# A PSUM bank for each copy of the first x tile, the activation table load behind w1's issues, the last w1 gradient in halves, and a new set of planner constants

## The chip, the cores and the metric

The kernel runs on one core of one Trainium2 chip. The time is the device time of one execution in microseconds (us). The engines are TensorE (PE, with its weight loads PEld), VectorE (DVE), ScalarE (ACT), GpSimd (POOL) and SyncE (SP, which here only issues DMAs).

## The reference

The kernel computes the output and all gradients of a small speech network: two strided convolutions, each followed by GELU, and a joint of the frames with eight label states.

```python
B, T, D, K, U = 2, 16000, 256, 3, 8          # all inputs bf16
# forward
h = gelu(conv(x, w1))[:, ::2]                # kernel width 3
f = gelu(conv(h, w2))[:, ::2]                # [2, 4000, 256]
fe = f @ w_f;  ge = g @ w_g
j = tanh(fe[:, :, None] + ge[:, None])       # [2, 4000, 8, 256]
out = j @ w_o                                # [2, 4000, 8, 256]
# backward, from grad_out of the shape of out
return out, grad_x, grad_w1, grad_w2, grad_g, grad_w_f, grad_w_g, grad_w_o
```

## The kernel before

**Tiling.** The 8000 output frames of both batches are cut into chunks: the first has 256 frames, fifteen have 512 (of these, one holds the border of the two batches), the last has 64. One chunk runs through three stages. `stage_a` loads x transposed into `XC` (by a DMA transpose; for the first chunk rows are loaded and TensorE transposes them, in `rows_xc`), makes both convolutions with GELU and its derivative (`conv_gelu`: g_sq, g_s, G1o, G1e, G2), and fe. `stage_j` handles the eight label states in four pairs (`pair(up)`): JT is tanh(fe+ge), `OUT` is JT times w_o, `GOT` is grad_out transposed by DMA, NGZ/ZS/NGP collect the gradient through tanh, `JR` is JT with frames on partitions, and `gwo` sums w_o's gradient into the bank `GWO`. For the first two chunks JR comes from TensorE transposes of JT (L688), later from a DVE add and an ACT tanh (L694, L699). `stage_de` goes back through both convolutions: GN, GH, their DMA transposes GNR and GHR, the weight gradients (`wgrad`, accumulated in ACC1, ACC2 and ACCF) and the gradient of x (`GX`).

**The order of the work** is made at build time by a planner, `Flow`. Each step is an `op` with an engine (or a choice of two, mostly ACT or DVE), a modelled cost, the tiles that it reads and writes, and a due time (`at`, or `F.now`). Times of `at` are in frames: a chunk of 512 frames is 512 long, `dt` is the chunk's length, `q` a quarter of it, one pair's time. `Flow.issue` runs a model of the engines: of the steps whose inputs are done and whose buffer is free it takes the one that can start first, and among those that can start at the same time the one due first. The result is a fixed list of instructions for each engine. On the chip an engine runs its list in order and waits where an input is missing. SP's list is chosen in the same model, with one DMA ring: `TURN` holds the pause between kinds of transfers (T transpose, L load, S store), `BACKLOG` how far SP may run ahead.

**PSUM.** Seven banks are handed out as class `ps` in any order; the eighth is GWO. An ACT and a DVE instruction that read the same bank run one after the other on the chip; the model before does not know that.

**Start.** L1174 zeroes a tile, 20 matmuls on it (`warm_up`) run while the first x travels. ACT issues the loads of w1 (three), w_f, w_g and w_o, and then loads its function table with a small GELU (L1175). In `rows_xc` the halves of x come one after the other: eight TensorE transposes (L388) into one bank, two copies of that bank into XC (L324 on ACT, L329 on DVE), and filler matmuls (`unread`, FILL of them) behind each half's transposes.

**End.** `last_w1(i)` makes the gradients of w1's three taps for the last two chunks at once. Its result, 256 x 256, fills one bank, a DVE instruction adds ACC1 to it (L901, `acc_add` with `final`), and a store of 128 KB follows. The last chunk's four GX copies (L326, L331) and two stores are due around it (`late`).

Of the kernel before, what the change touches and what calls it, by code (L numbers as in the profile page):

```python
# [20 lines left out]
class Buf:  # L21


    def __init__(self, cls, shape, dtype, name):
        self.cls, self.shape, self.dtype, self.name = cls, shape, dtype, name
        self.t, self.slot, self.log, self.users, self.seq, self.born, self.free = None, None, [], 0, None, None, 0.0

# [8 lines left out]
class Flow:  # L36
# [4 lines left out]
    TURN = {"TT": 250.0, "TL": 750.0, "SL": 900.0, "LL": 200.0, "TS": 250.0, "LS": 250.0, "SS": 400.0}  # L41
# [65 lines left out]
    def issue(self):  # L107
# [14 lines left out]
        while left:  # L122
            best = None
            for e, lst in avail.items():
                t, wake, cand, near = T[e], self.WAKE[e], None, []
                for o in lst:
# [11 lines left out]
                    if s is None:  # L138
                        continue
                    s = max(s, t)  # L140
# [36 lines left out]
            for b in o.bufs:  # L177
                b.users -= 1
# [32 lines left out]
def kernel(  # L211
# [28 lines left out]
    KT = 2  # L240
# [94 lines left out]
    def dma(q, out, in_, r, w, bytes_, new=(), transpose=False, load=False, at=None, after=(), behind=(), land=1500.0, lag=0.0):  # L335
# [28 lines left out]
    FILL = (6, 7)  # L364
# [10 lines left out]
    def rows_xc(c, XC, at):  # L375
# [7 lines left out]
        for h in range(2):  # L383
            ps = psum(BF16)

            def trs(e, h=h, ps=ps):
                for n in range(8):
                    nc.tensor.transpose(out=ps[:, n * P:(n + 1) * P], in_=XL[:, 4 * h + n // 2, n % 2 * P:(n % 2 + 1) * P],  # L388
                                        identity=ident[:])
            turned = op("PE", c_pe([P] * 8), trs, r=[(XL, h), ident], w=[ps], new=[ps], at=at)  # L390
            unread(FILL[h], [turned])
            for k in range(2):
                evac(lambda h=h, k=k: XC[:, 1 + 4 * h + 2 * k:3 + 4 * h + 2 * k].rearrange("p j k n -> p (j k n)"),
                     lambda k=k, ps=ps: ps[:, k * 512:(k + 1) * 512], 512, r=[ps], w=[(XC, ("m", 2 * h + k))], f=0.5, at=at)
# [71 lines left out]
    def conv_gelu(g_, jobs, rd, h_buf, pre, ho, gname, gcls, gshape, gsave, news):  # L466
# [39 lines left out]
        late = F.now + CW * ({2: 0.17, 1: 0.61}.get(g_, 0.25))  # L506
# [34 lines left out]
    def stage_a(g_, t0, dt):  # L541
# [25 lines left out]
        F.now = t0 + 0.08 * dt  # L567
# [3 lines left out]
        F.now = t0 + 0.10 * dt  # L571
# [3 lines left out]
        F.now = t0 + 0.20 * dt  # L575
# [15 lines left out]
        F.now = t0 + 0.38 * dt  # L591
# [9 lines left out]
        F.now = t0 + 0.55 * dt  # L601
        if NTR <= g_ < LAST:
            fe_rows(g_)
        F.now = t0 + 0.84 * dt
# [49 lines left out]
    def stage_j(g_, t0, dt):  # L654
# [7 lines left out]
        def pair(up):  # L662
# [4 lines left out]
            for j in range(2):  # L667
                for mt in range(KT):
                    for k_, (lo, hi, b) in enumerate(parts_of(c)):
# [4 lines left out]
                           new=[JT] if j == 0 and mt == 0 and k_ == 0 else [], at=tu - q * (1.00 - (2 * j + mt) / 4))  # L674
            npart = len(parts_of(c))
            for h in range(max(nb // 2, 1)):
                na = min(nb, 2)
                JR = buf("jr", [P, 2, 2, D], BF16, "JR")
                th = tu + q * (h / 2 - 0.56)
# [636 lines left out]
```

## Time and profile before

| | |
|---|---|
| Time, median of 3 runs (lowest, highest) | 771.13 us (770.98, 774.52) |
| Profiled execution, its own time | 771.4 us |
| Profiled execution, span | 769.6 us |
| Granted TensorE clock | 1.00 |
| Busy: PE, DVE, ACT, POOL | 761.3, 720.8, 699.9, 96.3 us |
| First x transpose, first convolution | 5.16, 7.55 us |
| Last TensorE matmul starts, last DVE row starts | 764.94, 765.57 us |
| DMA | 183.82 MB, mean 239 GB/s |

The span runs from the first instruction of the program to its last; the execution's own time has 1.8 us around it. Busy times are unions of rows; a TensorE row includes its way through the array, so that rows overlap, and the work of TensorE is read from the spacing of starts.

### The profile page before, as it was taken

How to read it: one execution, taken by the hardware profiler on the slowest of the kernel's cores; microseconds unless marked ns; L12 is line 12 of the kernel's file. 1: busy time of each engine (PE TensorE's matmuls, PEld its weight loads, DVE VectorE, ACT ScalarE, POOL GpSimd, SP SyncE). 2: the span in 40 equal slices, each digit the busy share in tenths (PEclk: the TensorE clock that was granted, in tenths of full speed). 3: DMA queues.
4: the chain of work that ended last, by engine and by line, in shares of the span. 5: the costliest groups of instructions: out<-in, count | busy, mean ns of one | idle time of the engine just before them, and what ended most of it. 6: DMA issues, size and time to landing. Idle time of an engine off the chain costs nothing.

```text
span 769.6 us, 15273 instructions
## 1 busy us (share of the span) xinstructions
PE 761.3 (99%) x5603; PEld 531.2 (69%) x5603; DVE 720.8 (94%) x1486; ACT 699.9 (91%) x1121; POOL 96.3 (13%) x222
## 2 busy tenths in 40 slices
PE   9999999999999999999999999999999999999997
PEld 7766667575776757767576675766757667677775
DVE  5999999999999999999999999989999999999984
ACT  6989999989999999999999989989999999999842
POOL 2010110101102011020100201102021020211000
PEclk9999999999999999999999999999999999999999
DMA  8999999999999999999999999999999999889773
GB/s 204 225 237 256 239 262 241 250 242 270 230 260 243 238 263 220 281 234 239 269 240 283 207 255 255 242 286 217 268 241 218 257 216 286 213 222 249 192 202 105
DMA packets 394200, 183.82 MB, mean 239 GB/s; under 512 B 317985, under 2 KB 387276, under 8 KB 392204
## 3 DMA queue, kind: packets, MB, share of 16 engines
q1 hardware_dynamic: 391578, 181.64, 101.6%
q10 hardware_dynamic: 2450, 1.18, 0.6%
q8 instruction: 44, 0.72, 0.4%
q14 instruction: 32, 0.26, 0.1%
q0 software_dynamic: 96, 0.02, 0.0%
HBM read 52.99 MB, written 50.35 MB: 134 GB/s over the span
## 4 chain that ended last, share of the span: by engine, by line
PE 88%; DVE 0%; DVEq 0%; ACT 0%; issue 0%
PE ps L315 74%; PE GWO L315 13%; PE psb L616 1%; DVE NGZ L739 0%; DVE GN L754 0%; DVEq L1311 0%; DVE JR L694 0%; PE psb L878 0%; PE psb L814 0%; ACT GX_SB L326 0%; PE psb L1150 0%; DVE GX_SB L331 0%
## 5 line engine op out<-in xcount | busy, mean ns | idle before, releaser
L670 ACT ACTIVATE JT<-FE,GE 128x512 bf16<-128x512 bf16 (+3 forms) x272 | 175.7, 692 | 0.0
L315 PE MATMUL ps<-WO,JT 128*128 128x256 bf16 x1000 | 148.1, 273 | 0.1
L315 PE MATMUL ps<-GOT,WOT 128*128 128x512 bf16 (+1 forms) x516 | 147.3, 372 | 0.0
L739 DVE SCALAR_TENSOR_TENSOR NGZ<-JSQ,ps 128x512 f32<-128x512 bf16 (+2 forms) x238 | 147.3, 630 | 0.0
L730 ACT ACTIVATE JSQ<-JT 128x1024 bf16<-128x1024 bf16 (+1 forms) x124 | 129.8, 1050 | 9.6 <-DVE NGZ L739 6.8
L315 PEld LDWEIGHTS <-JT 128*128 128x128 bf16 x1000 | 97.7, 98 | 59.2 <-DVE W1T L329 0.3
L699 ACT ACTIVATE JR<-JR 128x1024 bf16<-128x1024 bf16 x112 | 119.4, 1066 | 17.4 <-DVE JR L694 17.2
L315 PE MATMUL GWO<-GO_R,JR 128*128 128x256 bf16 x1000 | 129.6, 273 | 0.8 <-DVE JR L329 0.8
L324 ACT CAST OUT_SB<-ps 128x512 bf16<-128x512 f32 x192 | 112.6, 593 | 8.5 <-PE ps L315 7.0
L754 DVE TENSOR_TENSOR ZS<-ZS,NGZ 128x1024 f32<-128x1024 f32 (+1 forms) x96 | 113.4, 1182 | 0.4
L315 PEld LDWEIGHTS <-JR 128*128 128x128 bf16 x1000 | 97.5, 98 | 21.6 <-DVE JR L329 1.1
L315 PEld LDWEIGHTS <-W 128*128 128x128 bf16 x636 | 60.1, 98 | 59.8 <-issue 0.5
L315 PE MATMUL ps<-W1T,GH 128*128 128x256 bf16 (+2 forms) x506 | 94.6, 325 | 0.0
L315 PE MATMUL ps<-XC,W 128*128 128x512 bf16 (+2 forms) x432 | 86.5, 351 | 0.1
L315 PE MATMUL ps<-GHR,XR 128*128 128x256 bf16 (+1 forms) x736 | 83.3, 273 | 0.0
L315 PEld LDWEIGHTS <-XR 128*128 128x128 bf16 (+1 forms) x756 | 73.7, 98 | 8.9 <-issue 0.2
L694 DVE TENSOR_TENSOR JR<-FER,GEB 128x1024 bf16<-128x1024 bf16 x112 | 76.7, 685 | 3.3 <-PE GWO L315 3.0
L910 DVE TENSOR_TENSOR ACC<-ACC,ps 128x512 f32<-128x512 f32 x87 | 57.7, 679 | 12.1 <-PE ps L315 12.0
L315 PEld LDWEIGHTS <-GH 128*128 128x128 bf16 (+1 forms) x506 | 49.5, 98 | 25.8
L326 ACT ACTIVATE GX_SB<-ps 128x512 bf16<-128x512 f32 (+1 forms) x94 | 55.0, 610 | 9.7 <-DVE STAGE L901 5.0
L315 PEld LDWEIGHTS <-WOT 128*128 128x128 bf16 x516 | 49.6, 98 | 19.4 <-issue 0.2
L497 ACT ACTIVATE g_sq<-ps 128x512 bf16<-128x512 f32 (+2 forms) x102 | 57.8, 567 | 2.6 <-PE ps L315 2.6
(140 smaller groups left out, 1000.0 us busy)
## 6 DMA issues: line engine op xcount, KB each, us to landing
GO_R<-in_grad_out_dram SPq DMA_DIRECT2D x60, 512.0 KB, 5.9
out_dram<-OUT_SB SPq DMA_DIRECT2D x60, 512.0 KB, 5.1
XR<-in_x_dram SPq DMA_DIRECT2D x15, 1088.0 KB
out_dram<-GX_SB SPq DMA_DIRECT2D x30, 512.0 KB, 3.3
GOT<-GO_R SPq DMA_TRANSPOSE x65, 5.1
GO_R<-in_grad_out_dram SPq DMA_DIRECT2D x4, 256.0 KB, 4.1
out_dram<-OUT_SB SPq DMA_DIRECT2D x4, 256.0 KB, 5.0
out_dram<-STAGE SPq DMA_DIRECT2D x6, 128.0 KB
```

What stands on the lines that cost most here:

```text
L315: nc.tensor.matmul(ps_ap, lhsT=lhsT, rhs=rhs, start=start, stop=stop)
L324: nc.scalar.copy(out=dst(), in_=src())
L326: nc.scalar.activation(out=dst(), in_=src(), func=ACT.Copy, scale=scale)
L497: op("ACT", c_act(W, True), lambda e, mt=mt, ps=ps: nc.scalar.activation(out=sq[:, 0:nb, mt, :n_], in_=blk(ps, c), func=ACT.Square, scale= ...
L616: nc.tensor.transpose(out=ps[:n_, (a * KT + kt) * P:(a * KT + kt + 1) * P], in_=FE[:, kt, a * n_:(a + 1) * n_], identity=ident[:])
L670: op("ACT", c_act((hi - lo) * nb, ptr=True), lambda e, j=j, mt=mt, lo=lo, hi=hi, b=b: nc.scalar.activation(out=cut(JT[:, j, mt, :W], lo, h ...
L694: op("DVE", c_dve(na * 2 * D, 0.5), lambda e, h=h, na=na, JR=JR: nc.vector.tensor_tensor(out=JR[:n_, 0:na], in0=S["FER"][:n_, 2 * h:2 * h ...
L699: op("ACT", c_act(na * 2 * D), lambda e, na=na, JR=JR: nc.scalar.activation(out=JR[:n_, 0:na], in_=JR[:n_, 0:na], func=ACT.Tanh), r=[JR], ...
L730: nc.scalar.activation(out=JSQ[:, :, :W], in_=JT[:, j, :, :W], func=ACT.Square)
L739: nc.vector.scalar_tensor_tensor(out=cut(Z[:, d2, :W], lo, hi), in0=cut(JSQ[:, d2, :W], lo, hi), scalar=1.0, in1=cut(ps[:, :W], lo, hi), o ...
L754: nc.vector.tensor_tensor(out=o_, in0=i0, in1=i1, op=ALU.add)
L910: op("DVE", c_dve(512), lambda e: nc.vector.tensor_tensor(out=acc_ap().rearrange("p k d -> p (k d)"), in0=acc_ap().rearrange("p k d -> p ( ...
```

## The change

It has five parts.

1. `rows_xc`: each copy of the first x gets a bank of its own, with four transposes; the first four of a half are copied by DVE, the second four by ACT. FILL goes from (6, 7) to (5, 5).
2. The activation that loads ACT's table is issued behind the three w1 loads, ahead of w_f's, w_g's and w_o's.
3. `last_w1(2)` is made in two halves of 128 rows, each with a bank, a DVE instruction of 256 columns and a store of 64 KB (the first by ACT, the second by SP). The last chunk's second pair of GX steps is due at 4e3 instead of 1e4, ahead of `last_w1(2)` (5e3).
4. The planner's model: a reader of a PSUM bank starts after the reader on another engine is done (`touch`), other `TURN` pauses, another latency of SP's transfers and other costs of loads, stores and transposes.
5. Due times of many steps: JT, JR, gwo, JSQ, the stages of `stage_a`, the loads of grad_out (GO), its transposes (GOT) and x (XC).

```diff
     WAKE = {"PE": 45.0, "ACT": 25.0, "DVE": 25.0, "POOL": 60.0, "SP": 60.0}
-    TURN = {"TT": 250.0, "TL": 750.0, "SL": 900.0, "LL": 200.0, "TS": 250.0, "LS": 250.0, "SS": 400.0}
+    TURN = {"TT": 70.0, "TL": 150.0, "SL": 150.0, "LL": 0.0, "TS": 430.0, "LS": 800.0, "SS": 480.0, "LT": 50.0, "ST": 150.0}
...
+                    for b in o.bufs:
+                        for x, f in b.touch.items():
+                            if x != e and f + wake > s:
+                                s = f + wake
...
-                    begin = max(dma_free + gap, s + 1300.0)
+                    begin = max(dma_free + gap, s + 1900.0)
...
             for b in o.bufs:
+                if b.cls == "ps":
+                    b.touch[e] = o.done
...
         if transpose:
-            c, work = 1020.0 + bytes_ / 1100.0, bytes_ / 234.0
+            c, work = 640.0 + bytes_ / 430.0, bytes_ / 240.0
         else:
-            c, work = 600.0, bytes_ / 384.0
+            c, work = 600.0, bytes_ / (325.0 if load else 430.0)
...
-    FILL = (6, 7)
+    FILL = (5, 5)
...
         for h in range(2):
-            ps = psum(BF16)
-            def trs(e, h=h, ps=ps):
-                for n in range(8):
...
-            turned = op("PE", c_pe([P] * 8), trs, r=[(XL, h), ident], w=[ps], new=[ps], at=at)
+            for k in range(2):
+                ps = psum(BF16)
+                def trs(e, h=h, k=k, ps=ps):
+                    for n in range(4):
...
+                turned = op("PE", c_pe([P] * 4), trs, r=[(XL, h), ident], w=[ps], new=[ps], at=at)
+                evac(..., f=0.5, at=at, eng=("ACT", "DVE")[1 - k])
             unread(FILL[h], [turned])
...
-        late = F.now + CW * ({2: 0.17, 1: 0.61}.get(g_, 0.25))
+        late = F.now + CW * ({2: 0.21, 1: 0.57}.get(g_, 0.25))
...            # stage_a: dues after the first convolution, in shares of a chunk
-        0.08  0.10  0.20  0.38  0.55  0.84
+        0.11  0.22  0.27  0.54  0.63  0.75
...            # pair(up)
-                           JT:  at=tu - q * (1.00 - (2 * j + mt) / 4))
+                           JT:  at=tu - q * (0.59 - (2 * j + mt) / 4))
-                JR:  th = tu + q * (h / 2 - 0.56)
+                JR:  th = tu + q * (h / 2 - 0.84)
-                gwo: at=tu + q * (h / 2 + 0.49) + DEFER.get((g_, up), 0.0)
+                gwo: at=tu + q * (h / 2 + 0.02) + DEFER.get((g_, up), 0.0)
-                    JSQ: at=F.now - q * 0.16
+                    JSQ: at=F.now - q * 0.36
...            # stage_de
-        F.now = t0 + dt * 0.04
+        F.now = t0 + dt * 0.14
-                    late = F.now + (1e4 if cp else 3e3) if c.last else None
+                    late = F.now + (4e3 if cp else 3e3) if c.last else None
...            # last_w1
+        if i == 2:
+            for d2 in range(KT):
+                ps = psum()
+                ... all terms of both chunks into ps[:, 0:D], one op
+                ... DVE: t_[:, 0:D] = -ACC1[:, i, d2] - ps[:, 0:D]
+                dma("ACT" if d2 == 0 else "SP", ..., bytes_=65536)
+            return
...
-    op("ACT", 1400.0, <Gelu on warm>, r=[(warm, 0)], w=[(warm, 1)], at=BIG + 5.0)
+    wact = lambda after: op("ACT", 1400.0, <Gelu on warm>, r=[(warm, 0)], w=[(warm, 1)], at=BIG - 0.5, behind=after)
...
+    wact(w1l[-1:])       # after the loop that issues w1, before w_f
...
-                load_go(k, up, t0 + Wk * (up // 2 * 2 / UP - 0.60), ...)
-                load_got(k, up, t0 + Wk * (up / UP - 0.71))
+                load_go(k, up, t0 + Wk * (up // 2 * 2 / UP - 0.48), ...)
+                load_got(k, up, t0 + Wk * (up / UP - 0.61))
-            load_xc(k + 1, t0 - Wk * 0.21)
+            load_xc(k + 1, t0 - Wk * 0.18)
```

More of the change, by code (lines that the diff above doesn't have):

```diff
@@ L574, in stage_a @@
         pad_tail(g_, HT, "e", (oE, oE + nb))
[L575 removed]
+        F.now = t0 + 0.27 * dt
         def conv2(mt, h):
@@ L733, in pair @@
                     op(("ACT", "DVE"), (c_act(KT * W), c_dve(KT * W, 0.5)), jsq,
-                       r=[(JT, (j, mt, k_)) for mt in range(KT) for k_ in range(npart)], w=[JSQ], new=[JSQ], at=F.now - q * 0.16)
+                       r=[(JT, (j, mt, k_)) for mt in range(KT) for k_ in range(npart)], w=[JSQ], new=[JSQ], at=F.now - q * 0.36)
                 Z = ZS if first else NGZ
@@ L1106, in last_w1, with half @@
     def last_w1(i):
+        two = [w1_terms(g_, i) for g_ in (LAST - 1, LAST)]
+        if i == 2:
+            for d2 in range(KT):
+                ps = psum()
+                lst = [x_ for t_ in two for x_ in t_]
+                def half(e, d2=d2, ps=ps, lst=lst):
+                    for k, (lhs, rhs, _) in enumerate(lst):
+                        mm(ps[:, 0:D], lhs(d2), rhs(), k == 0, k == len(lst) - 1)
+                rd = []
+                for _, _, l in lst:
+                    rd += [b for b in l if b not in rd]
+                op("PE", c_pe([D] * len(lst)), half, r=rd, w=[ps], new=[ps])
+                t_ = stage()
+                op("DVE", c_dve(D), lambda e, d2=d2, ps=ps, t_=t_: nc.vector.scalar_tensor_tensor(
+                    out=t_[:, 0:D], in0=ACC1[:, i, d2], scalar=-1.0, in1=ps[:, 0:D], op0=ALU.mult, op1=ALU.subtract),
+                   r=[(ACC1, i), ps], w=[t_], new=[t_])
+                dma("ACT" if d2 == 0 else "SP", lambda d2=d2: out_2[i][d2 * P:(d2 + 1) * P, :], lambda t_=t_: t_[:, 0:D],
+                    r=[t_], w=[], bytes_=65536)
+            return
         ps = GWO if i == 0 else psum()
         pv = GWO.t[:].rearrange("p k v -> p (k v)") if i == 0 else None
-        two = [w1_terms(g_, i) for g_ in (LAST - 1, LAST)]
         n = [0, KT * sum(len(t_) for t_ in two)]
```

35 lines of the change are left out of this document (18 added, 17 removed).

## The prediction

> **What bounds the kernel now.** I read the engine totals first, then the chain of waits, the waits of TensorE, the windows by stage, and last the timeline of the first 13 us, of 30 to 42 us and of the last 15 us.
>
> ```profile
> PE 761.3 (99%) x5603; PEld 531.2 (69%) x5603; DVE 720.8 (94%) x1486; ACT 699.9 (91%) x1121; POOL 96.3 (13%) x222
> ```
>
> TensorE is busy throughout. A busy row may still hide gaps, so I look at the spacing of starts. In the tail, 16 matmuls of 256 columns start at 759.38 us and the next group starts at 761.12 us: 1.74 / 16 = 109 ns each. The same reading gives 216 ns for 512 columns (12 from 740.00 to 742.59) and 56 ns for a 128-column transpose (8 from 32.29 to 32.73). By the code, one full chunk issues 224 matmuls of 256 columns, 104 of 512 and 8 transposes: 224 x 0.109 + 104 x 0.216 + 8 x 0.056 = 24.4 + 22.5 + 0.4 = 47.3 us. The chain of waits (start us, us, what) shows the period:
>
> ```profile
> 196.90 7.39 PE ps L315 x56
> ...
> 244.25 7.39 PE ps L315 x56
> ...
> 291.60 7.39 PE ps L315 x56
> ```
>
> The same piece comes back every 47.35 us. The period equals the matmul sum, so from about 90 us to 750 us there is no gap that any order of the same instructions could close. What can be gained lies before 90 us and after 750 us. All waits of TensorE on record (us in total, times, longest); the second is the start of the program:
>
> ```profile
> PE psb L688 <- ACT JT L670: 1.3, 1, 1.3
> PE ps L315 <- DVE g_sq L1174: 1.1, 1, 1.1
> PE GWO L315 <- DVE JR L329: 0.8, 1, 0.8
> PE ps L315 <- DVE GN L754: 0.2, 1, 0.2
> ```
>
> Going through the starts one by one and taking off 109, 216 or 56 ns, the excess is 3.9 us between 18 and 91 us: 0.98 at 35.47 (the JR wait), 1.50 at 40.04 (the JT wait), 0.34 at 47.67, 0.31 at 19.20, the rest in pieces of 0.1 to 0.3. I call this the ramp. It lies where ScalarE, not TensorE, is full (columns: PE, PEld, DVE, ACT, POOL busy, clock, DMA share, GB/s):
>
> ```profile
> 20.00:47.00 27.00, 24.85 (x240) 20.53 (x238) 25.94 (x71) 26.94 (x49) 1.22 (x6) 1.00 1.15 238
> ...
> 90.00:137.00 47.00, 47.00 (x332) 31.96 (x330) 46.02 (x91) 46.80 (x73) 5.40 (x15) 1.00 1.09 251
> ...
> 232.00:279.00 47.00, 47.00 (x336) 32.40 (x335) 45.34 (x89) 43.77 (x67) 6.34 (x12) 1.00 1.08 254
> ```
>
> **The change part by part.** The sum is made against the profiled execution: span 769.6, own time 771.4, so 1.8 lies around the span. The median of the runs is 771.13, 0.3 lower. I subtract the sum from that median.
>
> *First x, banks and fill.* Today the eight transposes of a half go into one bank, and its two copies take turns on it:
>
> ```profile
> 4.47 1.28 ACT L1175 ACT_TABLE_LOAD   x1 [4.47 <-DMA W<-in_w_dram]
> 5.16 0.61 PE L388 MATMUL psb<-ident,XL 128*128 128x128 bf16 x8
> 5.88 0.57 ACT L324 COPY XC<-psb 128x512 bf16<-128x512 bf16 x1
> 6.26 0.61 PE L388 MATMUL psb<-ident,XL 128*128 128x128 bf16 x8
> 6.91 0.59 ACT L324 COPY XC<-psb 128x512 bf16<-128x512 bf16 x1 [0.46 <-PE psb L388]
> 7.53 0.42 DVE L329 COPY XC<-psb 128x512 bf16<-128x512 bf16 x1 [0.62 <-ACT XC L324]
> 7.55 3.02 PE L315 MATMUL ps<-XC,W 128*128 128x256 bf16 x24
> ```
>
> The last DVE copy waits for ACT's and ends at 7.95. The first convolution issues two matmuls at 7.55, then waits until 8.01. With a bank per copy: one filler less before the second half puts its transposes at 6.26 - 0.11 = 6.15; both halves of x have landed by 4.9 us (end of their packets 4.5), so they are no limit. DVE copies the first four from about 6.6 to 7.0, beside ACT, which takes the last four from 6.15 + 0.61 + 0.06 = 6.82 to 7.41. The convolution is free of its second wait at 7.47, not 8.01: 0.54 us. The five fillers after it end at 7.2 and don't delay it. The last slice of w1, whose packets end at 6.04, does not either.
>
> *Table load.* Load (1.28) and its small ACTIVATE (0.21) move ahead of the issues of w_f, w_g and w_o, so those go out some 1.5 us later, and the last, now at 4.05 because it waited for its queue, at about 4.8. Their packets end at 6.51, 7.25 and 8.78 today; the first reader, a transpose of w_o, starts at 10.68. Covered by over 1 us; without that cover up to 0.75 us. ACT is free for its first copy at 5.3, before 5.77. Cost nil. The Trainium skill, ScalarE: Activation LUTs, section "What ACT_TABLE_LOAD costs", speaks against this: it adds a drain of about 1.38 us to each load. By that, an estimate, ACT would be issuing until 6.6, its two copies would end at 7.8 and the gain shrink from 0.54 to 0.15. Here the ACTIVATE follows the load at 5.77, 0.02 us after its end, so the trace shows no such drain, at least behind the load.
>
> *Last gradient of w1.* Today the end is this:
>
> ```profile
> 764.61 0.60 PE L315 MATMUL ps<-GHR,XR 65*128 65x256 bf16 x4
> ...
> 765.22 0.42 DVE L331 TENSOR_SCALAR GX_SB<-ps 65x256 bf16<-65x256 f32 x1 [2.12 <-ACT GX_SB L326]
> 765.57 0.67 DVE L901 SCALAR_TENSOR_TENSOR STAGE<-ACC,ps 128x512 bf16<-128x512 f32 x1
> ...
> 766.27 0.40 ACTq L341 DMA_DIRECT2D out_dram<-STAGE  x1
> ```
>
> The matmuls end at 765.21, but DVE first finishes a gx copy and starts 0.36 late. The change moves the last gx matmuls (4e3 instead of 1e4) ahead of this gradient, so that copy is out of the way: -0.36. Then DVE handles 256 columns, not 512 (0.42 against 0.67): -0.25. The last store is 64 KB, not 128; packets of the last one take about 1.0 us, I count -0.1 to -0.4, say -0.1. TensorE's work is the same; no part of this gradient serves as filler today before GHR of the last chunk is there (758.64), so joining its two parts costs nothing. Sum: -0.7 us. The halves' stores go by ACT and SP, whose earlier issues are done by then.
>
> *Planner.* Costs and dues are new, so the order of every engine changes. In the ramp, bounds: -3.9 (all excess gone) to +3.0 (two more waits like the longest, 1.50). The JR copy that ended the 0.98 wait ran behind an OUT_SB copy and a ZS add on DVE; its due goes from 0.56 to 0.84 of a pair's time ahead, so I take that wait as gone. The 1.50 wait stays: ACT, full there, ran a 1.05 us tanh (L509) before the JT that TensorE wanted, and JT's due gets later (1.00 to 0.59), which does not help. Value: -1.0.
>
> In the steady chunks a gain is excluded by the period. Losses: tanh of JT ends 10 to 21 us before its first matmul there, and its due moves 0.41 x 11.84 = 4.9 us; JR's lead is 5.4 to 12 us, and shrinks by (0.47 - 0.28) x 11.84 = 2.2 us. Both stay covered. DVE (45.3 of 47) and ACT (43.8 of 47) have some room. Value 0, bound in the third rival. The planner's new rule that a reader of a bank waits for the reader on the other engine matches what the trace does already (DVE waits 10.5 us in all for ACT's read of a convolution's bank); it issues nothing by itself.
>
> Sum: -0.54 - 0.7 - 1.0 = -2.2 us: 771.13 - 2.2 = 768.9.
>
> **Rivals.** First: the whole ramp closes. For it: DVE's waits on ACT are now planned with, so more copies may go to DVE and free ACT. Against: ACT 26.94 of 27 and DVE 25.94 of 27 leave little. Time: 771.13 - 0.54 - 0.7 - 3.6 (of 3.9) = 766.3.
>
> Second: the ramp gets worse through the later JT. For it: the 1.50 wait is just that kind. Against: ACT's order there is full of work that is not urgent. With the bound +3.0: 771.13 - 1.2 + 3.0 = 772.9.
>
> Third, on the other side: a GOT transpose arrives late once in each chunk. GOT's due moves from 0.71 to 0.61 of a chunk, 4.7 us, and GO's from 0.60 to 0.48. SP's queue carries them behind stores and loads. The tightest of steady chunks today (SP issue and its TensorE reader):
>
> ```profile
> 213.30 5.04 SPq L339 DMA_TRANSPOSE GOT<-GO_R  x1
> ```
>
> It ends at 218.34, its reader starts at 225.03: 6.7 us, and transposes land 1.7 to 3.5 us after their issue ends. Spare is 3.2 to 5.0 us; it decides from there. If the whole 4.7 us come through, up to 1.5 us a chunk is lost, 14 times; with 0.5 us a chunk: 768.9 + 7 = 775.9, with 1.5: 789.9. Against: a due sorts what is ready, it does not hold back, and most pairs have 10 to 25 us.
>
> Fourth: only the edges work, or the earlier start is lost again to a full ACT: 771.13 - 0.7 = 770.4.
>
> **How the numbers follow.** About 0.5% (3.9 us) is what a measurement of this kernel can tell from no change: faster is below 767.3, slower above 775.0. Forecast 0.46 (its own range 767.0 to 770.2, by the ramp from -2.9 to +0.3), first rival 0.20, second 0.10, third 0.13, fourth 0.11. The first rival and a little of the forecast (0.04) make 0.24 faster. The third and 0.02 of the second, if its waits are more than two, make 0.15 slower. That leaves 0.61 the same. The range runs from 766.0, below which only part of the first rival lies, to 775.5, which leaves out most of the third: 766.0 to 775.5.
>
> **What would show it.** Right: the first convolution's third matmul near 7.5 us; both copies of a half side by side; TensorE's wait for JR gone and ACT's JT still the longest; the period 47.35 us; the last DVE row 0.4 us long and right behind the last matmul. Wrong: a period over 47.4 us, any TensorE wait that comes back in each chunk, a reader of w_o, w_f or w_g waiting for its load, or a ramp with new waits for JT.

## The result, and the profile after

The kernel after takes 774.62 us (median of 8 runs, 773.7 to 775.19), the kernel before 771.22 in the same job. The ratio is 1.0037, interval [1.0024, 1.005]: 3.4 us slower, where 2.2 us faster was forecast. The profiled execution has a span of 773.4 us and an own time of 775.19. Helper lines are 7 further down than before (L315 is now L322, L329 is L336, L670 is L677, L688 is L695).

All waits of TensorE on record (engine, tile, line, released by: us in total, times, longest):

```profile
PE GWO L322 <- DVE JR L336: 1.9, 2, 1.5
PE ps L322 <- DVE GH L1000: 1.5, 1, 1.5
PE psb L695 <- ACT JT L677: 1.4, 3, 0.7
PE ps L322 <- DVE g_sq L1201: 1.1, 1, 1.1
PE psb L1240 <- DMA WO<-in_w_o_dram: 0.8, 1, 0.8
PE ps L322 <- DVE GN L761: 0.5, 1, 0.5
PE ps L322 <- ACT GX_SB L333: 0.2, 1, 0.2
```

The JR wait, which the prediction took as gone, has doubled. The one long JT wait became three shorter ones. Three are new: a convolution that waits for DVE to free a bank (GH), w_o, and GX_SB.

The spacing of TensorE's starts, less 109, 216 or 56 ns each, gives the excess by stretch. It is the measure that I use throughout:

| us | 0 to 11 | 11 to 18 | 18 to 46 | 46 to 100 | 100 to 700 | from 700 |
|---|---|---|---|---|---|---|
| before | 2.41 | 0.73 | 3.08 | 0.89 | 0.20 | 0.93 |
| after | 2.99 | 1.27 | 4.35 | 2.91 | 0.20 | 1.37 |

So 3.3 us more excess lie between 18 and 100 us, in the ramp and what follows it. The steady chunks are as before. From the chain of waits (start us, us, what):

```profile
206.62 8.69 PE ps L322 x64
...
253.96 8.69 PE ps L322 x64
...
301.31 8.69 PE ps L322 x64
```

The same piece comes back every 47.35 us. The long starts of the ramp, and the one behind it, from TensorE's timeline (start us, us, operation, in brackets the idle time before it and who ended it):

```profile
36.77 1.05 PE L322 MATMUL GWO<-GO_R,JR 128*128 128x256 bf16 x8 [1.50 <-DVE JR L336]
...
38.54 0.23 PE L695 MATMUL psb<-ident,JT 128*128 128x128 bf16 x1 [0.66 <-ACT JT L677]
39.15 0.23 PE L695 MATMUL psb<-ident,JT 128*128 128x128 bf16 x1 [0.38 <-ACT JT L677]
39.76 0.90 PE L695 MATMUL psb<-ident,JT 128*128 128x128 bf16 x13 [0.38 <-ACT JT L677]
...
41.92 1.05 PE L322 MATMUL GWO<-GO_R,JR 128*128 128x256 bf16 x8 [0.39 <-DVE JR L336]
...
97.03 1.25 PE L322 MATMUL ps<-XC,W 128*128 128x512 bf16 x5 [1.54 <-DVE GH L1000]
```

The largest single new piece is the last one, 1.70 us of excess. It lies behind the ramp, and no experiment below isolates it.

The windows of this stretch show TensorE at 2.38 and 2.32 of 4 us, with DVE and ACT full; then ACT is idle for 1.21 us (columns: PE, PEld, DVE, ACT, POOL busy, clock, DMA share, GB/s). Before, DVE (28.00) and ACT (27.94) were busy for nearly all of the 28 us from 22 to 50; after, 26.94 and 26.78. The two sums are those of after and, below it, of before:

```profile
34.00:38.00 4.00, 2.38 (x20) 1.68 (x18) 4.00 (x13) 4.00 (x8) 0.00 (x0) 1.00 1.23 245
38.00:42.00 4.00, 2.32 (x24) 1.71 (x25) 4.00 (x9) 4.00 (x7) 1.46 (x3) 1.00 1.11 244
42.00:46.00 4.00, 4.00 (x42) 3.62 (x43) 4.00 (x14) 2.79 (x7) 0.00 (x0) 1.00 1.24 263
...
sum 28.00, PE 24.17 PEld 19.21 DVE 26.94 ACT 26.78 POOL 2.10; mean PE 3.45 PEld 2.74 DVE 3.85 ACT 3.83 POOL 0.30
...
sum 28.00, PE 25.68 PEld 21.07 DVE 28.00 ACT 27.94 POOL 1.60; mean PE 3.67 PEld 3.01 DVE 4.00 ACT 3.99 POOL 0.23
```

The start and the end, from the timelines. The two copies of the second half of x now overlap (DVE from 7.40, ACT from 7.62), and the last DVE row is half as wide as before. The first convolution's third matmul starts at 8.26, not near 7.5: the last of TensorE's first matmuls at half speed (213 ns for 256 columns) starts at 6.36 us here, at 4.67 before:

```profile
2.15 5.79 SPq L346 DMA_TRANSPOSE XC<-in_x_dram  x1
2.28 1.28 ACT L1202 ACT_TABLE_LOAD   x1 [2.28 <-issue]
...
3.58 0.21 ACT L1202 ACTIVATE g_sq<-g_sq 128x8 bf16<-128x8 bf16 x1
4.24 0.38 ACTq L348 DMA_DIRECT2D WG<-in_w_g_dram  x1
4.66 0.51 ACTq L348 DMA_DIRECT2D WO<-in_w_o_dram  x1
...
12.15 0.40 PE L1240 MATMUL psb<-ident,WO 128*128 128x128 bf16 x4 [0.82 <-DMA WO<-in_w_o_dram]
...
769.73 0.42 DVE L1129 SCALAR_TENSOR_TENSOR STAGE<-ACC,ps 128x256 bf16<-128x256 f32 x1 [0.46 <-PE ps L322]
```

### The profile page after: what moved, and what is told of

Same layout as the page of the kernel before. It is cut to its first block, busy times and chain, and to the rows that moved or that the text cites. A ratio compares the mean times of both kernels' runs of the same rounds, so it can differ in the third digit from the quotient of the medians.

```text
span 773.4 us, 15230 instructions
## 1 busy us (share of the span) xinstructions
PE 762.0 (99%) x5600; PEld 531.6 (69%) x5600; DVE 712.0 (92%) x1473; ACT 699.7 (90%) x1135; POOL 69.7 (9%) x222
## 4 chain that ended last, share of the span: by engine, by line
PE 90%; DVE 5%; ACT 3%; DMA 1%; issue 1%; ACTq 0%; DVEq 0%
PE ps L322 75%; PE GWO L322 13%; DVE NGZ L746 1%; DMA WO<-in_w_o_dram 1%; DVE ZS L761 1%; PE psb L623 1%; ACT JT L677 1%; DMA W<-in_w_dram 0%; DVE GH L979 0%; ACT g_sq L504 0%; ACT HT L506 0%; DVE G L508 0%; DVE GH L1000 0%; DVE JR L336 0%; ACT JSQ L737 0%
## 5 line engine op out<-in xcount | busy, mean ns | idle before, releaser
L677 ACT ACTIVATE JT<-FE,GE 128x512 bf16<-128x512 bf16 (+3 forms) x272 | 175.3, 723 | 0.0
L322 PE MATMUL ps<-WO,JT 128*128 128x256 bf16 x1000 | 148.6, 273 | 0.0
L322 PE MATMUL ps<-GOT,WOT 128*128 128x512 bf16 (+1 forms) x516 | 147.7, 373 | 0.0
L331 ACT CAST OUT_SB<-ps 128x512 bf16<-128x512 f32 x204 | 124.0, 625 | 16.8 <-PE ps L322 16.8
L322 PEld LDWEIGHTS <-JT 128*128 128x128 bf16 x1000 | 97.6, 98 | 59.3
L737 ACT ACTIVATE JSQ<-JT 128x1024 bf16<-128x1024 bf16 (+1 forms) x123 | 133.1, 1082 | 1.7 <-DVE NGZ L746 1.2
L706 ACT ACTIVATE JR<-JR 128x1024 bf16<-128x1024 bf16 x112 | 121.8, 1087 | 14.0 <-DVE JR L701 13.4
L322 PE MATMUL GWO<-GO_R,JR 128*128 128x256 bf16 x1000 | 129.6, 273 | 1.9 <-DVE JR L336 1.9
L322 PEld LDWEIGHTS <-JR 128*128 128x128 bf16 x1000 | 97.6, 98 | 16.8 <-DVE JR L336 2.4
L322 PEld LDWEIGHTS <-W 128*128 128x128 bf16 x636 | 59.9, 98 | 57.8 <-DMA XC<-in_x_dram 1.8
L322 PE MATMUL ps<-W1T,GH 128*128 128x256 bf16 (+2 forms) x506 | 96.9, 325 | 0.2 <-ACT GX_SB L333 0.2
L322 PE MATMUL ps<-XC,W 128*128 128x512 bf16 (+2 forms) x432 | 88.3, 351 | 1.5 <-DVE GH L1000 1.5
L322 PE MATMUL ps<-GHR,XR 128*128 128x256 bf16 x736 | 83.3, 273 | 0.0
L322 PEld LDWEIGHTS <-XR 128*128 128x128 bf16 (+1 forms) x756 | 73.7, 98 | 9.0 <-issue 0.2
L333 ACT ACTIVATE GX_SB<-ps 128x512 bf16<-128x512 f32 (+1 forms) x98 | 59.9, 633 | 17.0 <-PE ps L322 16.7
L322 PEld LDWEIGHTS <-WOT 128*128 128x128 bf16 x516 | 50.1, 98 | 25.9
L322 PEld LDWEIGHTS <-GH 128*128 128x128 bf16 (+1 forms) x506 | 49.0, 98 | 26.6 <-issue 0.5
L504 ACT ACTIVATE g_sq<-ps 128x512 bf16<-128x512 f32 (+2 forms) x102 | 60.1, 590 | 2.7 <-PE ps L322 2.7
```

Source lines behind the costliest of these rows:

```text
L322: nc.tensor.matmul(ps_ap, lhsT=lhsT, rhs=rhs, start=start, stop=stop)
L331: nc.scalar.copy(out=dst(), in_=src())
L333: nc.scalar.activation(out=dst(), in_=src(), func=ACT.Copy, scale=scale)
L504: op("ACT", c_act(W, True), lambda e, mt=mt, ps=ps: nc.scalar.activation(out=sq[:, 0:nb, mt, :n_], in_=blk(ps, c), func=ACT.Square, scale= ...
L677: op("ACT", c_act((hi - lo) * nb, ptr=True), lambda e, j=j, mt=mt, lo=lo, hi=hi, b=b: nc.scalar.activation(out=cut(JT[:, j, mt, :W], lo, h ...
L706: op("ACT", c_act(na * 2 * D), lambda e, na=na, JR=JR: nc.scalar.activation(out=JR[:n_, 0:na], in_=JR[:n_, 0:na], func=ACT.Tanh), r=[JR], ...
```

## The experiments

All were timed beside the kernel before, 5 to 12 executions each. "Fixed order" means that the planner's finished sequence of operations and buffers is written into the kernel, so that one part can be changed and every other operation stays in its place. Times below are medians; the difference is to before in the same job; the last two columns are the excess of TensorE.

| run | us | to before | ratio, interval | 18 to 46 | 46 to 100 |
|---|---|---|---|---|---|
| edges_only | 771.33 | -0.46 | 0.9994 [0.9985, 1.0003] | 3.13 | 0.90 |
| plan_only | 775.38 | +3.59 | 1.0045 [1.0027, 1.0062] | 5.46 | 1.61 |
| table_only | 772.28 | +0.49 | 1.0008 [0.9999, 1.0017] | | |
| bank_only | 770.78 | -1.01 | 0.9989 [0.9979, 0.9999] | 3.09 | 0.90 |
| after_ramp | 775.82 | +4.32 | 1.0056 [1.0044, 1.0069] | 6.67 | 1.71 |
| bank_end | 770.35 | -1.15 | 0.9981 [0.9972, 0.999] | 3.07 | 0.90 |
| bank_end_ramp | 770.41 | -1.09 | 0.9989 [0.998, 0.9998] | 3.15 | 1.04 |
| table_sp | 771.35 | -0.15 | 0.9998 [0.9989, 1.0007] | 3.20 | 0.76 |
| after_land1300 | 772.92 | +1.28 | 1.0017 [1.0008, 1.0025] | 5.13 | 0.13 |
| before_land1900 | 774.34 | +2.70 | 1.0035 [1.0022, 1.0048] | 2.89 | 3.74 |
| model_only | 772.64 | +1.00 | 1.0022 [1.0009, 1.0034] | 3.78 | 1.21 |
| dues_only | 774.14 | +2.50 | 1.0042 [1.0027, 1.0056] | 5.36 | 0.68 |
| h_before_after | 774.64 | +3.12 | 1.0039 [1.0026, 1.0052] | 3.30 | 1.17 |
| h_after_before | 773.53 | +2.01 | 1.0027 [1.0016, 1.0037] | 5.31 | 0.59 |
| before_less | 771.05 | -0.47 | 0.9997 [0.9988, 1.0006] | 2.13 | 0.78 |
| after_less | 773.53 | +2.01 | 1.0028 [1.0018, 1.0038] | 3.58 | 0.96 |
| before_more | 773.22 | +1.30 | 1.0016 [1.0007, 1.0025] | 4.96 | 0.60 |
| edges_sp | 770.57 | -1.35 | 0.9979 [0.997, 0.9987] | 3.23 | 0.75 |

The last two columns need care. In five of the profiled executions the granted clock of TensorE falls to 0.50 for 3.4 us inside the ramp: in h_after_before from 38.01, plan_only from 38.69, after_ramp from 38.86, dues_only from 39.33, after_land1300 from 40.98. The starts within that time make 1.51, 1.64, 1.62, 1.77 and 1.66 us of their excess from 18 to 46 us. A window of plan_only shows it (the third number from the end is the clock):

```profile
38.00:42.00 4.00, 3.62 (x24) 2.92 (x25) 4.00 (x12) 2.98 (x5) 1.46 (x3) 0.59 1.74 271
```

In the other profiles, those of before and after too, the clock is 1.00 there. So the column "18 to 46" mixes waits and clock, and rows with and without the low clock are not alike. The low clock is not what makes the new order slow. The profiled execution of after lost its time at the full clock. And 3.4 us at 0.50 take the mean clock of an execution to 0.998, so that executions with a mean of 0.999 or more did not have it: h_after_before took 773.50 and 773.69 us in two such executions, and 773.04 to 773.69 in the five at 0.996 and 0.997 (the eighth, at 0.998, took 773.91); plan_only took 775.29, 775.67 and 776.06 in three such executions, and 773.85 and 775.38 in the two at 0.996 and 0.997. All six executions of dues_only have 0.995 or 0.996, so for that run the two can't be told apart. What makes the clock fall, no run here tested.

### Which part of the change

Theory O: the new order of the ramp costs the time. Theory S: the start does (late w_o, TensorE's clock). All four have a fixed order.

```diff
edges_only:  before's order; parts 1, 2 and 3 of the change put in
plan_only:   after's order; parts 1, 2 and 3 taken back
table_only:  before's order; part 2
bank_only:   before's order; part 1
```

> The order of before is kept for every engine, written out as a fixed list; only the bank split with the fillers, the place of the table load and the halves of the last gradient are in. Theory O (the 3.4 us are lost by the new order between 18 and 98 us): 0.2 to 1.3 us faster than before, ramp excess 3.9 us as before. Theory S (they are lost at the start, by the late w_o and the half clock): 0.5 to 3 us slower than before, with TensorE waiting about 1 us for w_o near 12 us.

> The order of the changed kernel is kept as a fixed list, but its three edits at the start and the end are taken back (one bank for a half of x, fillers 6 and 7, table load last, last gradient in one piece). Theory O: 4 to 5 us slower than before, ramp excess near 7 us. Theory S: within 1 us of before.

> Order of before as a fixed list, only the table load moved behind the issues of w1. If the moved load lets the transposes of x into the queue ahead of w_g and w_o: SP's first x transpose issued near 2.1 us instead of 3.7, w_o landed near 12 us instead of 9, and a TensorE wait of 0.5 to 1 us for w_o; the time 0 to 1 us over before. If the late w_o came from something else in the changed kernel: no such wait, the time as before.

> Order of before as a fixed list, only the banks of the first x and the fillers (5, 5). Banks as predicted: first convolution complete 0.3 to 0.54 us earlier than in before and the time 0 to 0.5 us lower. If the fewer fillers keep the clock at half speed: matmul starts 213 ns apart beyond 5 us, and the first convolution later than in before.

Theory O held. The new order by itself costs 3.59 us (4 to 5 were expected), the three edges by themselves gain 0.46, which its interval does not tell from nothing, and 3.59 - 0.46 = 3.1 is nearly the 3.4 of the whole. In bank_only the copies run side by side, and the first convolution's 24th matmul starts at 9.74, not 10.30 us. The two profiles are alike up to there: the last matmul at half speed starts at 4.66 in one and at 4.67 in the other. The median fell by more than the 0 to 0.5 us expected, 1.01 with an interval from 0.1 to 1.6. The two copies of the second half:

```profile
6.54 0.42 DVE L329 COPY XC<-psb 128x512 bf16<-128x512 bf16 x1 [0.57 <-PE psb L389]
...
6.76 0.59 ACT L324 COPY XC<-psb 128x512 bf16<-128x512 bf16 x1 [0.20 <-PE psb L389]
```

The table load eats part of what the banks bring. Its +0.49 is at the edge of what the interval tells from nothing, but the wait is plain: in table_only w_o's issue moved from 4.05 to 4.60 us, its last packet from 8.78 to 11.30, and TensorE stood idle for it until 12.21. From the waits of table_only:

```profile
PE psb L1213 <- DMA WO<-in_w_o_dram: 0.9, 1, 0.9
```

### The late w_o

Before, SP's first transposes of x went out at 3.69 us, behind w_f and w_g. With the table load moved they go out at 2.15, ahead of w_g and w_o. table_sp keeps the moved table load and lets SP issue w_g and w_o ahead of those transposes.

```diff
-    wload("ACT", WG, ...)        # ACT, behind the table load
-    wload("ACT", WO, ...)
+    wload("SP", WG, ...)         # SP, ahead of its transposes of x
+    wload("SP", WO, ...)
```

> Before's order with the table load behind w1's issues (as in the run of that edit alone: 772.28, w_o landed at 11.30 us and the tensor engine waited 1.05 us for it at 12.2), and with the loads of w_g and w_o issued by SP ahead of its transposes of x instead of by ScalarE behind the table load. If the late w_o comes from its place behind the long transposes, w_o lands before 9.5 us again, the wait near 12 us goes, and the median is 0.7 to 1.1 us below 772.28: 771.2 to 771.6 (at best 770.8, if the table load off ScalarE's path also starts the first convolution earlier). Rival (the late w_o comes from the queue's bandwidth, or the table load costs elsewhere): the wait stays over 0.5 us, the time over 771.9.

It held: 771.35, 0.15 below before, where table_only was 0.49 above (the 0.93 between their medians are of two jobs). SP issued w_o at 4.20 and the transposes at 4.61, and TensorE does not wait for it. The answer for the tile WO in the first 14 us (who waited for it: no one):

```profile
L1213 PE MATMUL psb<-ident,WO x4: 220/220/230, 10.4 to 10.5; 128*128 128x128 bf16 x4
L341 SPq DMA_DIRECT2D WO<-in_w_o_dram x1: 368/368/368, 4.2 to 4.2; - x1
its engine sat idle before it (us, times) until:
who waited for it (us, times):
```

So with the same bytes, ahead of the transposes, w_o is in time. That SP and not ACT issues it here is a second difference, which this run does not separate. The table load's new place shows no gain of its own: 0.15 below before, inside the interval.

### The two waits of the ramp, moved by hand

In the timeline of after, ACT ran three tanhs of the first chunk's activation gradient ahead of the gate products JT that TensorE wanted, and DVE ran the copy of JR (36.03) behind three sums:

```profile
31.71 1.17 ACT L516 ACTIVATE g_s<-g_s 128x1024 bf16<-128x1024 bf16 x1
...
33.12 1.19 ACT L516 ACTIVATE g_s<-g_s 128x1024 bf16<-128x1024 bf16 x1
34.08 1.17 ACT L516 ACTIVATE G<-G 128x1024 bf16<-128x1024 bf16 x1
...
36.01 0.85 ACT L677 ACTIVATE JT<-FE,GE 128x512 bf16<-128x512 bf16 x1
```

It looks like a plain case of two misplaced operations. after_ramp moves them in after's order, bank_end_ramp the same two in before's.

```diff
 after_ramp, ACT                       after_ramp, DVE
-tanh g_s, tanh g_s, tanh G            +copy JR
 FE, JSQ, FE, JT, JSQ, OUT_SB, JT x7    NGZ x2, ZS, JSQ, NGZ x2, ZS, NGZ
+tanh g_s, tanh g_s, tanh G            -copy JR
```

> The kernel after with its own order of issue written out, and only the ramp of it altered: on ScalarE the three 128x1024 tanh operations that ran at 31.71, 33.12 and 34.08 us (1.17 us each) go behind the eight gate products JT that they delayed, their five VectorE followers go behind the GOT sums, and on VectorE the copy of JR that ran at 36.03 goes up to just behind its transposes (done near 32.9). Theory O (the loss is the order of the ramp, these two places above all): the waits of 1.66, 0.83, 0.55 and 0.55 us between 36.7 and 40.4 shrink from 3.6 us to under 1.5, the ramp's excess in 18 to 46 us falls from 4.35 to 1.5 to 2.7, and the median is 772.0 to 773.3 against 774.6. Rival F (ScalarE and VectorE are simply full in the ramp, so that a wait taken out at 37 us comes back behind it): the excess before 46 us falls but that of 46 to 100 us (2.9) rises by as much, and the time stays within 0.5 us of 774.6.

> Before's order of issue, with the banks of the first x and the halves of the last gradient of w1, and the table load left where before has it. If the moved table load is what took the gain of these two away in the run with all three (771.33), this one shows both: 0.56 us at the start, and 0.3 to 0.7 at the end: 770.1 to 770.6 against 771.5 of before. If instead the banks or the halves give nothing when they are together (rival: the time saved at the start is lost again at the first store or at the ramp), it is 771.2 to 771.6.

> The kernel of bank_end, with two operations of before's ramp moved: on VectorE the copy of JR (34.73 us) goes ahead of the sum, the OUT_SB copy and the second ZS addition that it stood behind (so to 33.19), and on ScalarE the tanh at 38.33 goes behind the last JT. Theory O says that the same two places which cost the kernel after 3.4 us also cost the kernel before its two ramp waits of 0.98 and 1.50 us: the first goes, the second falls to about 0.5, and the time is 1.5 to 2.2 us below that of bank_end: 768.0 to 769.0. Rival F (the engines are full, the wait comes back behind): within 0.5 us of bank_end.

Theory O fell here in its narrow form, and rival F (ACT and DVE are full) fits better. after_ramp is no faster than after: 4.32 against 3.40 above before, each in its own job, with intervals that overlap. ACT did little to pull JT forward (35.31, not 36.01, with a first convolution that ended 0.96 earlier); it waited. Its timeline in after_ramp:

```profile
30.46 0.60 ACT L331 CAST FE<-ps 128x512 bf16<-128x512 f32 x1
34.31 0.63 ACT L737 ACTIVATE JSQ<-JT 128x512 bf16<-128x512 bf16 x1 [3.25 <-DVE NGZ L746]
34.84 0.57 ACT L331 CAST FE<-ps 128x512 bf16<-128x512 f32 x1
35.31 0.72 ACT L677 ACTIVATE JT<-FE,GE 128x512 bf16<-128x512 bf16 x1
```

A square of JT stands in ACT's queue ahead of the JT that TensorE waits for. It needs a JSQ buffer, there are two, and the NGZ sums on DVE read them first. The tanhs had filled that hole. Moved back, they ran at 41 us and later, where ACT had other work, and 3.25 us of ACT were lost.

In bank_end_ramp the JR wait did go, and the time did not follow (0.06 us more than bank_end). Its waits:

```profile
PE psb L688 <- ACT JT L670: 1.6, 3, 0.9
...
PE ps L315 <- DVE GN L754: 0.3, 1, 0.3
PE ps L315 <- DVE OUT_SB L329: 0.2, 1, 0.2
```

Of the 0.8 of JR, 0.3 came back as JT (1.3 to 1.6, 0.9 of it right in front of the transposes that follow), 0.1 as GN and 0.2 as OUT_SB.

bank_end itself came in as expected, 770.35, 1.15 us below before. The medians do not show what the halves add to the banks: bank_only alone was 1.01 below, in another job.

### Which constants

Theory G: GOT's first product is late (27.93 us before, 30.21 after), because the planner now thinks that SP's transfers begin 1900 ns after the issue, and squares, sums and gate products follow it. Rival M: any new order of the ramp costs.

```diff
 after_land1300 (from after; before_land1900 is the reverse, from before)
-                    begin = max(dma_free + gap, s + 1900.0)
+                    begin = max(dma_free + gap, s + 1300.0)
 model_only: before with part 4 of the change
 dues_only:  before with part 5 of the change
```

> The kernel after with one number of the planner's model set back: a transfer of SP begins 1300 ns after its issue, as before, and not 1900. Moving the tanhs and the JR copy by hand did not help, and ScalarE then sat idle for 3.25 us before its squares of JT at 34.3, waiting for a JSQ buffer that the NGZ sums on VectorE had not read yet. So theory G: what is late in the ramp is the first product GOT x WOT (27.93 us before, 30.21 after), because SP issued GOT 3.4 us later (18.62, 21.99) and the planner, which thinks each transfer lands later still, put GOT's product 10 places further back in TensorE's order; sums, squares and gate products follow it through two JSQ buffers. With 1300 back, the planner puts that product at nearly its old place (28 to 28.5), the excess of 18 to 100 us falls from 7.3 to 4 to 5.5, and the median is 771.5 to 773. Rival M (the place of GOT's product is one of many things; any new order of the ramp costs as much): 774 or more.

> The kernel before with that one number changed, 1300 to 1900. Theory G: GOT's first product moves back by 1 to 2 us (to about 29.5), the ramp grows, and the median is 772.5 to 774. Rival M (the number by itself does little; the loss comes from all constants and due times together): within 0.7 us of before, 770.8 to 772.2.

> The kernel before with the planner's model of banks and ring alone (the turn times, the wait for a bank touched by another engine, the landing and ring constants), none of the new due times. Theory G: the model's later landing is in it, so GOT's first product comes at 29.5 to 30 and most of the loss of the ramp is here: 773 to 775. Rival M: half of the loss here, half with the due times: 772.5 to 773.

> The kernel before with the new due times alone and the planner's old model. Theory G: GOT's first product stays at about 28 and the time within 1 us of before (770.5 to 772.3). Rival M: 772.5 to 773.

The two single-number runs came in as G said (before_land1900 0.3 above its range), and the number is a large lever: alone it costs 2.70 us, taken back it returns 2.1 of after's 3.4 (3.40 against 1.28). But the mechanism did not hold in the other two. In dues_only GOT's first product starts at 27.99, as early as before, and 2.50 us are still lost, more than either theory gave. model_only, with the 1900 in it, loses only 1.00 (772.64, in the range of M). Its product starts at 29.23, but 0.87 of that is a later start of the whole (the first convolution's 24th matmul at 11.17, not 10.30), so the product moved back by 0.43 only. So the place of that one product is not the whole: dues_only, and after_land1300 with it at 28.23, have it early and still lose 2.50 and 1.28. Model and due times come to 1.00 + 2.50 = 3.50 together, near the 3.59 of plan_only, though each has an interval of about 1 us either way.

What the slow orders share is idle time on engines that were full before. Idle of DVE and ACT together, out of 2 x 28 us from 22 to 50 us: before 0.06, bank_end 0.08, model_only 0.38, bank_end_ramp 0.69; dues_only 1.86, plan_only 2.15, before_land1900 2.26, after 2.28, after_ramp 6.37. The exception is after_land1300, with 3.14 idle and only 1.28 lost; it then has no excess behind the ramp (0.13 against 0.89), and 1.50 of its 3.14 is DVE waiting until 44.46 for TensorE, which ran at the low clock from 40.98 to 44.39. This is a likeness, not a cause shown: table_only, late by w_o, has 1.18 idle. One window of before_land1900, where ACT had nothing to do for 1.71 us:

```profile
42.00:46.00 4.00, 4.00 (x43) 3.63 (x42) 4.00 (x14) 2.29 (x4) 0.00 (x0) 1.00 0.93 208
```

### Which stretch, and whether load bounds it

h_before_after has before's order for 342 operations, up to the second chunk's first convolution, and after's for the rest; h_after_before the reverse (326 operations). Both have the start and end of before. before_less and after_less leave seven steps out, so that the first chunk's gradient is another, and before_more does four steps twice. TensorE's instructions are the same in these three.

```diff
 before_less, after_less: ACT -tanh g_s, -tanh G; DVE -tensor_scalar x5
 before_more:             ACT +JSQ (29.85) x2;    DVE +copy JR (23.53), +copy OUT_SB (33.53)
```

> Before's start and end edges, and one hybrid order: before's order of issue up to the first convolution of the second chunk (342 operations, about 50 us), and from there the order of the kernel after. Theory F (ScalarE and VectorE are both full through the ramp, 22 to 50 us; an order that leaves one of them idle there, or passes work over to the next stretch, pays for it; the loss is made before 50 us): close to before, plus the 0.45 us that all kernels with the new due times show after 700 us: 771.6 to 772.8. Rival L (the loss is made in the stretch behind the ramp, where the after kernel waited 1.70 us at 97 us): 773 or more.

> The opposite hybrid: after's order up to the first convolution of the second chunk (326 operations), with before's start, and before's order from there. Theory F: the loss of the run with all of after's order (775.38) stays, less 0.5: 774 to 775.5. Rival L: 772.5 or less.

> The kernel before with its own order, seven in-place steps of the first chunk's activation gradient left out: two 128x1024 tanhs on ScalarE (at 38.33 and 40.40 us, 1.0 us each) and five tensor-scalar steps on VectorE (0.33 each: 35.93, 36.26, 36.59, 38.73, 42.23), so the gradient of that chunk is another. TensorE's instructions are the same. Theory F: the two engines bound the ramp, so 1.5 to 2 us less work on each takes 1.0 to 2.2 us off the time (769.3 to 770.5). Rival P (TensorE's order and its due times bound the ramp, the engines are only in its way at single places): under 0.5 us, as when the places were moved by hand.

> The kernel after with its own order and the same seven steps left out (two of the three tanhs at 33.12 and 34.08 us; of the VectorE steps three stand at 37.83 to 39.7 us and two between 26 and 30 us). Theory F: 1.5 to 2.5 us less than 774.6, so 772.1 to 773.1, and the difference to before_less stays over 2 us, since it is the order that leaves the engines idle. Rival P: 774 or more. If instead it comes within 1 us of before_less, the loss of the new order was these tanhs ahead of the gate products after all.

> The kernel before with its own order, four steps of the ramp done twice, the second time with the same result: on ScalarE the two squares of JT at 29.85 us (0.52 us apart, so 1.04 us more), on VectorE the copy of JR at 23.53 and the copy of OUT_SB at 33.53 (0.60 us each, 1.2 us more). TensorE's instructions are the same. Theory F (ScalarE and VectorE are full from 22 us on and TensorE waits for them at 35 and 40 us, so what is added to them ahead of that is added to the time): 0.8 to 1.4 us more than before, 772.3 to 773. Rival P (the ramp is bound by TensorE's order and single waits): under 0.4 us more.

after's order up to 50 us costs 2.01 us without the rest; its excess from 18 to 46 us (5.31) is near that of plan_only (5.46), 1.5 and 1.6 of it at the low clock. The time is 0.5 us under what F gave, and 1.0 above rival L's 772.5 (the loss is made behind the ramp). The opposite hybrid went against F: 774.64, where F gave 771.6 to 772.8 and L 773 or more. Its profiled execution took 773.17, with an excess almost like before's, but four of its six runs took 774.5 or more, and none of those has a profile. The two hybrids lose 2.01 and 3.12, together more than the 3.59 of the whole order, so the loss does not split at 50 us. after's order up to 50 us makes about 2 us by itself; what its order behind 50 us costs, and why, is not settled.

The load: before_more lost 1.30 us for 1.04 us more on ACT and 1.2 on DVE, within what F gave and far from rival P's under 0.4 (TensorE's order and single waits bound the ramp). The waits of before_more: JT 1.6 us instead of 1.3, and a new one of 1.4 us for ACT's FE copy, which stands behind the doubled squares:

```profile
PE psb L688 <- ACT JT L670: 1.6, 2, 1.3
PE ps L315 <- ACT FE L324: 1.4, 1, 1.4
PE ps L315 <- DVE g_sq L1174: 1.1, 1, 1.1
PE GWO L315 <- DVE JR L329: 0.7, 1, 0.7
```

Taking work out returned less than F said: 0.47 us in before (excess of the ramp 3.08 to 2.13; inside the interval, and P gave under 0.5) and 1.4 in after (3.40 against 2.01; 773.53, between the ranges of F and P), for 1.7 to 2 us less work on each engine. The JT wait of before_less fell from 1.3 to 0.4, but its JR wait at 35.45 is ahead of all that was left out, and stayed. So F holds one way: the work put on ACT and DVE ahead of TensorE's waits was paid; what was taken away helped only the waits behind it.

### The version that the runs point to

```diff
 edges_sp: before's order; parts 1, 2 and 3; w_g and w_o issued by SP as in table_sp
```

> Before's order with all three edge edits (banks of the first x, table load behind w1's issues, halves of the last gradient of w1), and w_g and w_o loaded by SP ahead of its transposes of x. The sum of the single runs: banks and halves together were 1.15 below before, and the table load cost nothing once w_o was not late (0.15 below before): 770.0 to 770.6. If w_g and w_o on SP get in the way of the first x when the first convolution starts earlier, 771 or more.

770.57 us, in the range expected and 1.35 below before: ratio 0.9979 [0.997, 0.9987]. bank_end, without the table load, is as good (0.9981 [0.9972, 0.999]). Both beat the kernel before and the kernel after.

## Why the prediction was wrong

**The planner's term is the step that failed.** It stood at -1.0 and measured +3.59 (plan_only). "I take that wait as gone" was read from JR's due time alone; but the copy ran at 36.03, behind three sums on DVE, and its wait went from 0.98 to 1.66. "The 1.50 wait stays" was too mild: it became 0.83, 0.55 and 0.55. The bound of +3.0, "two more waits like the longest", was just too small: the excess from 18 to 100 us rose by 3.29 to 7.26, in nine pieces over 0.15 us and not in two more; the largest, 1.70 at 97 us, is a wait for GH that the prediction does not name. The deeper error is that I judged single due times, when the prediction's own window (ACT 26.94 of 27, DVE 25.94 of 27) showed two nearly full engines. A new order there moved all waits at once: taking out one by hand returned nothing (bank_end_ramp 0.06 above bank_end), and adding 1.04 and 1.2 us of work cost 1.30. That the idle time which the new order opens on ACT and DVE is what costs the rest fits most of the runs, but h_before_after went against it, and why the new order costs 3.59 and not more or less stays open. The second rival had the sign and in part the place, at a chance of 0.10, and its 772.9 were 1.7 us too low. Its cause, the later JT, had little part: TensorE's waits for JT went from 1.3 to 1.4 us, those for JR from 0.8 to 1.9.

**Steady chunks: right.** Value 0; the period is 47.35 us as before, and no GOT transpose is late in each chunk, so the third rival fell.

**Not foreseen behind them:** 0.45 us from 700 us on, in two places (720.8 and 722.3 us) at the start of a gradient of x, the second of which waits 0.2 us for GX_SB. The kernels with the new due times have it (dues_only 1.38, plan_only 1.38), model_only does not (0.94).

**First x: right by itself.** -0.54 forecast; the convolution's 24th matmul starts 0.56 us earlier in bank_only, and the medians differ by 1.01 [0.1, 1.6], so that the size is right by the profile and not resolved by the times. In after the gain was hidden by the longer half speed of the first matmuls (8.26 for the third matmul, where about 7.5 was named). The Trainium skill, ScalarE: Activation LUTs, section "What ACT_TABLE_LOAD costs", puts a drain of about 1.38 us beside the load at every switch to another table set; in after too the ACTIVATE follows 0.02 us behind the load (3.56 to 3.58), so no run here shows one behind it.

**Table load: "cost nil" was wrong** by 0.9 us of wait in the profile and 0.5 us at the median, the latter at the edge of the interval. Issue at about 4.8 was right (4.66). The "cover of over 1 us" was counted from packets as they flowed before. I did not ask what else would go out while ACT loads its table: SP's transposes of x, 1.5 us earlier than before, in front of w_o.

**Last gradient: right by the profile.** -0.7 forecast. The last matmul's end to the last DVE row's end fell from 1.03 to 0.46 us, and from there to the end of the span from 3.35 to 3.25: -0.67. No pair of times shows it: bank_end and bank_only differ by 0.14, in two jobs.

**The sum:** the edges gave -0.46 where -1.24 was forecast, the table load being most of the difference; the planner turned the sign.

## What to carry to other kernels

Where the windows show two helper engines full and the tensor engine waiting for them, don't price a reordering by the wait it takes away: name what each full engine runs in its place, and look for holes that the new order opens. Here a wait removed by hand came back under other names. A step that is moved ahead of loads can let another queue's transfers past those loads; price who goes first, not the issue times. Look at the clock in each window before two runs' waits are compared. A model constant of a planner is not a small edit: one of them (1300 to 1900 ns) moved this kernel by 2.7 us.

## What the runs showed of the hardware

A load that ACT issues behind transposes of SP can be late by far more than its issue: in table_only w_o was issued 0.55 us later than before but behind transposes of x, and its last packet came 2.5 us later (8.78 to 11.30). In before the transposes went out at 3.69 us, though SP had issued its load of w2 by 2.11; why, no run here tested.

The clock of the first matmuls rises at a time that changes from run to run. Nine profiles start TensorE with the same instructions, the first matmul at 1.06 us, and have the table load where before has it; the last matmul at half speed (203 to 213 ns for 256 columns) starts at 3.60 us in h_after_before, 4.67 in before and 6.79 in h_before_after, and the first convolution's third matmul at 7.46, 8.01 and 8.99. So the first 11 us of two profiles should not be compared without it. The clock column does not tell: it reads 1.00 from 0 to 11 us in dues_only, where the last matmul at half speed starts at 4.88.

The granted clock can also fall in the middle of a run: to 0.50 for 3.4 us between 38 and 45 us, in five of twenty profiles. The spacing of starts then shows excess that is no wait, and the time of the execution did not follow it in h_after_before and plan_only, which ran both ways.
